# Attention and feed-forward on one core: the first two query blocks of batches 0 and 1 ahead of their later blocks, with feed-forward pieces cut to match

## The chip, the core and the metric

The kernel runs on one core of a Trainium2 chip. The core has five engines, each with an instruction queue of its own that is worked off in order: TensorE (PE in the profile), VectorE (DVE), ScalarE (ACT), GpSimd (POOL) and SyncE (SP). SP does no arithmetic; it issues DMAs. An engine that has to wait for another waits with everything that stands behind in its queue. The metric is the device time of one execution in microseconds: median 402.34 us of three runs (401.5 to 403.08).

## What is computed

A forgetting attention over 8 batches, 8 heads, 576 positions, 64 features, and then a bilinear feed-forward over its 4608 output tokens:

```python
scores = scale * np.matmul(q, k.transpose(0, 1, 3, 2))
cum = np.cumsum(log_f, axis=-1)
decay = cum[:, :, :, None] - cum[:, :, None, :]
scores = np.where(causal, -1000000000.0, scores + decay)
attn = softmax(scores)
attn_out = np.matmul(attn, v)
x = attn_out.transpose(0, 2, 1, 3).reshape(B * S, H * D)   # 4608 x 512
out = ((x @ w_a) * (x @ w_b)) @ w_out                      # w_a, w_b: 512 x 1536
```

## The kernel before

**Recording and order.** The program first records about 2300 operations, each a small function with an engine (or a choice of engines), and then emits them in the order of a table of numbers, ORDER; the string CHOICE gives the engine where there is a choice. Nothing is scheduled when it runs: each engine gets its instructions in the order of the table, and semaphores are set for the data and the buffers. So ORDER decides what stands ahead of what in every queue.

**Attention.** A number t counts pairs of heads, four to a batch (batch b has t = 4b to 4b+3), and u counts half batches (two pairs). The 576 query rows of a head are five blocks i = 0 to 4 (the last of 64 rows), and a causal block i needs keys 0 to i only. They are worked on in four groups g: blocks 1 and 0 together (g = 0), 2, 3 and 4. `qk_group` (L389) puts the scores of one group of one half batch into PSUM; `do_max` (L483), `do_exp` (L539, ACT), `do_recip` (L554) and `do_norm` (L561, POOL) make P of it. In batches 0 to 2 ("direct") the decay is added by PE, and the maximum is a DVE reduction (L488); from batch 3 on DVE adds the decay from a tile `spread` (L512). P is kept as blocks of 128x128 and has to be transposed for P times V: by a DMA on SP's queue (`do_tr`, L583), or by PE against an identity with an eviction by ACT or DVE (`pe_tr`, L591). Parts of P are called A0 (blocks 0 and 1, 6 squares), A1 (block 2, 6 squares), B (blocks 3 and 4, 13 squares), and A is A0 and A1 together. `values` (L788) records the transposes and P times V: in batches 0 and 1 apart for rows (0, 1), rows (2, 3) and block 4 (L623, L636); in the later batches all at once (L611, L613). `turns` (L785) names the parts that PE transposes. The result is evicted into xT, the transposed input of the feed-forward.

Batches 0 and 1 are recorded by `attention_by_blocks` (L765), which goes group by group over both halves, so that their first blocks can be finished before their later ones.

**Feed-forward.** `ffn(t0, n)` (L922) is one piece of n tokens from token t0 on (batch b holds tokens 576b to 576b+575). It has 12 steps fb: four matmuls psa and four psb (L874), a copy of psa by ACT or DVE (L138 or L142), a product by DVE into ht (L890). Then, for each 128 tokens, three parts of four matmuls pso (L899), a copy and a store. Psa, psb, pso, the transposes by PE and P times V share one ring of four PSUM banks ("ff"). A piece needs the attention of all its tokens. The pieces before are (0, 256), (256, 256), (512, 256), (768, 384), and then seven from token 1152 on with 512 tokens (the last 384). `chain` (L918) keeps the recorded order of all feed-forward matmuls.

**Other work.** q, k and v are loaded by SP (`load_qk`, L288; `load_v`, L272), cast mostly by POOL (L140, L142) and q and k transposed by DVE (L302). The three weights are loaded by POOL's queue (`weights`, L355), w_a and w_b in two pieces each (512 and 1024 columns), w_out in three. Forty `filler` operations (L175) of four small matmuls each have no use but to keep PE busy.

## Time and profile before

| what | value |
|---|---|
| runs | 401.5, 403.08, 402.34 us; median 402.34 |
| span of the profiled execution, first to last instruction | 400.7 us |
| median of the runs over this span | 1.6 us |
| mean granted TensorE clock | 0.986 |
| busy: PE, DVE, ACT, POOL | 383.2, 315.3, 250.0, 253.6 us |
| instructions: PE, DVE, ACT, POOL | 4040, 907, 757, 424 |
| DMA | 78.22 MB in 148311 packets |

The time of the profiled execution is known by its span alone; the runs stand 0.8 to 2.4 us above it. "Busy" of PE counts a matmul until its modelled end, and ends overlap the next matmul, so a busy PE need not be at its peak. Where the text speaks of full pace it goes by the distance between starts of matmuls.

### The profile page before, as it was taken

What the parts mean: (1) busy time and instruction counts of PE and PEld (TensorE: products, weight loads), DVE (VectorE), ACT (ScalarE), POOL (GpSimd) and SP (SyncE); (2) the same over time, 40 slices, a digit from 0 to 9 for tenths busy, and PEclk for the clock granted to TensorE, in tenths of its full rate; (3) what the DMA queues carried; (4) which work ended last, traced back from release to release, by engine and by line L of the source; (5) the groups of instructions that cost most, each with busy time, mean ns of one, the idle gap of its engine ahead of it and who ended that gap; (6) DMA issues with size and microseconds to landing.
All of it is one profiled execution on the core that took longest, in us unless ns stands there. A gap on an engine that the chain in (4) does not pass through costs nothing.

```text
span 400.7 us, 11076 instructions
## 1 busy us (share of the span) xinstructions
PE 383.2 (96%) x4040; PEld 212.0 (53%) x4040; DVE 315.3 (79%) x907; ACT 250.0 (62%) x757; POOL 253.6 (63%) x424
## 2 busy tenths in 40 slices
PE   8598799998999999999999999999999999999996
PEld 7466576765855544454445454544444444444553
DVE  8989798976778988997988889898969892373560
ACT  5798766666667778758785777577868673300011
POOL 3889876887397876897896849787968553000000
PEclk9889999998999999999999999999999999999999
DMA  7999989989999999999999999999997729000102
GB/s 282 240 186 289 204 177 224 213 150 215 208 301 208 227 171 330 201 277 212 295 187 286 211 255 273 233 241 190 276 187 218 157 66 202 28 2 36 71 0 79
DMA packets 148311, 78.22 MB, mean 195 GB/s; under 512 B 130592, under 2 KB 133408, under 8 KB 148256
## 3 DMA queue, kind: packets, MB, share of 16 engines
q1 hardware_dynamic: 144272, 72.53, 77.4%
q0 software_dynamic: 3696, 4.72, 7.0%
q8 instruction: 31, 0.51, 0.5%
q10 hardware_dynamic: 288, 0.26, 0.2%
q14 instruction: 24, 0.20, 0.1%
HBM read 49.69 MB, written 9.58 MB: 148 GB/s over the span
## 4 chain that ended last, share of the span: by engine, by line
PE 79%; DMA 9%; DVE 4%; POOL 2%; ACT 2%; issue 2%; SPq 0%; POOLq 0%; DVEq 0%; ACTq 0%
PE pso L899 22%; PE psa L874 22%; PE psb L874 21%; PE sc L401 8%; DMA wa<-in_moe_w_a_dram 5%; PE pv L611 2%; DVE st L488 2%; DMA k<-in_k_dram 1%; PE pv L613 1%; PE sc L636 1%; DMA PTB<-spread 1%; DMA PTB<-PB 1%; DVE qT L302 1%; PE pv L623 1%; ACT PB L550 1%
## 5 line engine op out<-in xcount | busy, mean ns | idle before, releaser
L874 PE MATMUL psa<-xT,wa 128*128 128x512 f16 (+2 forms) x528 | 116.2, 343 | 2.3 <-DMA wa<-in_moe_w_a_dram 1.7
L874 PE MATMUL psb<-xT,wb 128*128 128x512 f16 (+2 forms) x528 | 116.2, 343 | 0.1
L899 PE MATMUL pso<-wout,ht 128*128 128x512 f16 (+1 forms) x444 | 98.4, 374 | 0.0
L567 POOL TENSOR_SCALAR PA<-PA,st 128x128 f16<-128x128 f16 (+2 forms) x162 | 76.0, 482 | 31.8 <-DVE st L559 20.4
L890 DVE TENSOR_TENSOR ht<-psb,a 128x512 f16<-128x512 f32 (+2 forms) x132 | 76.2, 589 | 22.0 <-PE psb L874 15.0
L512 DVE CUSTOM_DVE_ANT_0 S<-sc,spread 128x128 f32<-128x128 f32 (+3 forms) x160 | 86.7, 567 | 7.7 <-PE sc L401 5.4
L138 ACT CAST a<-psa 128x512 f16<-128x512 f32 (+2 forms) x85 | 43.5, 515 | 55.9 <-PE psa L874 53.8
L874 PEld LDWEIGHTS <-wa 128*128 128x128 f16 x528 | 50.1, 99 | 45.5 <-issue 3.7
L874 PEld LDWEIGHTS <-wb 128*128 128x128 f16 x528 | 50.4, 99 | 41.5 <-issue 1.7
L567 POOL TENSOR_SCALAR PB<-PB,st 128x512 f16<-128x512 f16 (+1 forms) x84 | 58.7, 712 | 15.7 <-DVE st L559 14.6
L550 ACT ACTIVATE PA<-S,st 128x256 f16<-128x256 f32 (+2 forms) x120 | 59.9, 502 | 12.5 <-DVE st L512 12.4
L899 PEld LDWEIGHTS <-ht 128*128 128x128 f16 x444 | 41.7, 98 | 46.8 <-issue 1.3
L488 DVE TENSOR_REDUCE st<-sc 128x2 f32<-128x512 f32 (+7 forms) x68 | 46.3, 723 | 6.0 <-PE sc L401 5.3
L401 PE MATMUL sc<-kT,qT 32*128 32x128 f16 (+5 forms) x960 | 41.7, 272 | 5.5 <-ACT PA L550 2.1
L550 ACT ACTIVATE PB<-S,st 128x512 f16<-128x512 f32 x40 | 28.5, 714 | 7.9 <-DVE st L512 7.9
L401 PEld LDWEIGHTS <-qT 32*128 32x128 f16 (+1 forms) x960 | 18.6, 96 | 26.7 <-issue 14.4
L142 DVE CAST a<-psa 128x512 f16<-128x512 f32 (+2 forms) x47 | 26.2, 560 | 7.2 <-PE psa L874 6.6
L559 DVE RECIPROCAL st<-st 128x2 f32<-128x2 f32 x128 | 18.5, 157 | 14.0 <-ACT PA L550 8.7
L142 POOL CAST k<-k 128x1152 f16<-128x1152 f32 (+1 forms) x15 | 20.5, 1367 | 8.9 <-DMA k<-in_k_dram 8.9
L138 ACT COPY osb<-pso 128x512 f32<-128x512 f32 (+1 forms) x22 | 12.4, 570 | 19.9 <-PE pso L899 15.1
L138 ACT CAST xT<-pv 128x512 f16<-128x512 f32 (+2 forms) x39 | 17.0, 446 | 11.8 <-PE pv L636 5.8
L140 POOL TENSOR_SCALAR q<-q 128x1152 f16<-128x1152 f32 (+1 forms) x15 | 20.6, 1372 | 5.0 <-DMA q<-in_q_dram 4.2
(98 smaller groups left out, 491.5 us busy)
## 6 DMA issues: line engine op xcount, KB each, us to landing
spread<-cum_d SPq DMA_DIRECT2D x20, 576.0 KB, 5.9
out_dram<-osb SPq DMA_DIRECT2D x35, 256.0 KB, 3.8
q<-in_q_dram SPq DMA_DIRECT2D x15, 576.0 KB, 7.3
k<-in_k_dram SPq DMA_DIRECT2D x15, 576.0 KB, 5.2
v<-in_v_dram SPq DMA_DIRECT2D x32, 256.0 KB, 6.1
wout<-in_moe_w_out_dram POOLq DMA_DIRECT2D x3, 512.0 KB, 8.7
v<-in_v_dram SPq DMA_DIRECT2D x8, 128.0 KB, 7.2
wb<-in_moe_w_b_dram POOLq DMA_DIRECT2D x1, 1024.0 KB, 13.5
```

What stands on the lines that cost most here:

```text
L138: nc.scalar.copy(out=out_, in_=in_)
L140: ENG[e].tensor_scalar(out=out_, in0=in_, scalar1=0.125, scalar2=1.0, op0=MUL, op1=MUL)
L142: ENG[e].tensor_copy(out=out_, in_=in_)
L401: nc.tensor.matmul(out=dst, lhsT=lhsT, rhs=rhs, start=start, stop=stop, skip_group_check=True)
L488: nc.vector.tensor_reduce(out=m if i == 4 else st[:, 2 * i:2 * i + 2][:, h:h + 1] if isinstance(x, list) else m, in_=y, axis=AXX, op=MAX, ...
L512: nc.vector.tensor_tensor_reduce(out=o, in0=x, in1=y, scale=-1.0, scalar=3e38, op0=ADD, op1=MIN, accum_out=m)
L550: nc.scalar.activation(out=p_blocks(t, i)[:, :, h, :], in_=x.rearrange("p (j k) -> p j k", k=128), func=EXP, scale=sign, bias=st[:, c:c + ...
L559: nc.vector.reciprocal(out=st[:, 20 + 2 * i:22 + 2 * i], in_=st[:, 10 + 2 * i:12 + 2 * i])
L567: ENG[e].tensor_scalar(out=p, in0=p, scalar1=st[:, c:c + 1], scalar2=1.0, op0=MUL, op1=MUL)
L874: nc.tensor.matmul(out=o, lhsT=w16[:, db, 128 * fb:128 * fb + 128], rhs=tokens(db, t0, n), start=(db == 0), stop=(db == 3))
L890: nc.vector.tensor_tensor(out=ht[:, 0:n], in0=T.pop(("psb", t0, fb))[:, 0:n], in1=T.pop(("a16", t0, fb))[:, 0:n], op=MUL)
L899: nc.tensor.matmul(out=o, lhsT=T[("ht", t0, fb)][:, 128 * tb:128 * tb + 128], rhs=wout16[:, fb, c], start=(fb == 0), stop=(fb == 11))
```

## The change

Five things change, and the table ORDER with them.

1. PE now transposes part A0 of batches 0 and 1 only; A1 and B of batch 0 go to DMA transposes on SP's queue, and batch 1's A0 comes from there.
2. The early feed-forward pieces are (0, 256), (576, 256), (256, 320), (832, 320): the first two blocks of batch 0, the first two of batch 1, and then the rest of each. A piece of 320 tokens ends in a half block of 64 tokens, which `ff_out` computes as two matmuls of 64 rows and 256 columns into the two halves of one PSUM tile; two small stores follow. The piece for token pairs (PAIR), which nothing used, is gone.
3. w_a and w_b are loaded in three pieces of 512 columns, and the first no longer waits for the cast of v.
4. Only the first group of u = 1 still takes single PSUM banks of the ring "ff" for its scores (`single`); its groups 1 and 2 take two-bank tiles as the others do.
5. psa/psb and pso are chained apart, so a later piece's psa may stand ahead of an earlier piece's pso.

```diff
-        for lo, hi in ((0, 512), (512, DF)):
+        for lo, hi in ((0, 512), (512, 1024), (1024, DF)):
...
-            if not w_ops:
-                o.deps.append(v_ops[0][0])
...
-        return u == 1 and g < 3
+        return u == 1 and g == 0
...
-        return (b, part) in {(0, "A0"), (0, "A1"), (0, "B")}
+        return (b, part) in {(0, "A0"), (1, "A0")}
...
+            if half:
+                for x in range(2):
+                    nc.tensor.matmul(out=o[HP[x], :], lhsT=T[("ht", t0, fb)][:, 128 * tb:128 * tb + 64],
+                                     rhs=wout16[:, fb, 256 * x:256 * x + 256], start=(fb == 0), stop=(fb == 11),
+                                     skip_group_check=True)
+                continue
...
-    last_ff = []
-
-    def chain(o):
-        o.after.extend(last_ff[-1:])
-        last_ff.append(o)
+    last_ff = {"h": [], "o": []}
+
+    def chain(o, row):
+        o.after.extend(last_ff[row][-1:])
+        last_ff[row].append(o)
...
-        for tb in range(n // 128):
-            end = t0 + 128 * tb + 128 == NT
-            for c in (slice(0, 256), slice(256, 512)) if end else (slice(0, 512),):
+        for tb in range((n + 127) // 128):
+            end, half = t0 + 128 * tb + 128 == NT, n < 128 * tb + 128
+            for c in (slice(0, 256), slice(256, 512)) if end else (slice(0, 256 if half else 512),):
...
-    for t0, n in [(0, 256), (256, 256), (512, 256), (768, 384)] + [(1152 + 512 * n, 512 if n < 6 else 384) for n in range(7)]:
+    for t0, n in [(0, 256), (576, 256), (256, 320), (832, 320)] + [(1152 + 512 * n, 512 if n < 6 else 384) for n in range(7)]:
...
-        42-44 0 20 41 2 1 64 26 31 23 54 55 45 16 32 13 12 71 46 37 47 56 18 67 27 65 34 72 73 68 48 24 19
+        0 24 20 42 71 14 67 43 44 1 64 54 45 46 41 72 47 79 48-50 55 65 56 57 73 74 28 10 36 68 69 51 70 98
```

What the table does is seen in the queues. SP's queue from the load of batch 2's first k on, before (an xT target is a part A0 or A1 of batch 1, PTB a part B; L456 loads `spread`, L914 stores an output block):

```order
L288 DMA k_1459<-in_k_dram 128x1152
L583 DMA_TRANSPOSE xT_67<-S 128x6x128
L272 DMA v_1553<-in_v_dram 128x8x64 x2
L288 DMA k_1610<-in_k_dram 128x1152
L456 DMA spread_80<-cum_d 128x2x576
L288 DMA q_1619<-in_q_dram 128x1152
L583 DMA_TRANSPOSE xT_66<-PA 128x6x128
L914 DMA out_dram<-osb 128x512
```

The same place in SP's queue now, where the transposes are parts of batch 0 (PTB is part B of a pair, xT its part A1):

```order
L288 DMA k_1081<-in_k_dram 128x1152
L581 DMA_TRANSPOSE PTB<-PB_76 128x13x128
L581 DMA_TRANSPOSE xT_67<-PA 128x6x128
L272 DMA v_1261<-in_v_dram 128x8x64 x2
L272 DMA v_1375<-in_v_dram 64x8x64
L581 DMA_TRANSPOSE PTB<-PB_77 128x13x128
L581 DMA_TRANSPOSE xT_66<-PA 128x6x128
L272 DMA v_1479<-in_v_dram 128x8x64 x2
L581 DMA_TRANSPOSE xT_69<-spread_80 128x6x128
L581 DMA_TRANSPOSE xT_68<-spread_79 128x6x128
L581 DMA_TRANSPOSE PTB<-spread_80 128x13x128
L581 DMA_TRANSPOSE PTB<-spread_79 128x13x128
```

Eight DMA transposes of batch 0 (four of part B, four of A1) with the late v loads of batches 0 and 1 stand there now. The rest of batch 2's loads, which stood there, and batch 1's own transposes come behind them.

POOL's queue at the weights, before (L567 normalizes P; wa and wb are the weights w_a and w_b):

```order
L365 DMA wa_70<-in_moe_w_a_dram 128x4x512
L567 TENSOR_SCALAR PA<-PA,st 128x2x128 x2
L365 DMA wb_71<-in_moe_w_b_dram 128x4x512
L567 TENSOR_SCALAR PA<-PA,st 128x128
L142 CAST nv_74<-v_377 128x1024
L567 TENSOR_SCALAR spread_80<-spread_80,st 128x2x128
L365 DMA wb_71<-in_moe_w_b_dram 128x4x1024
L365 DMA wa_70<-in_moe_w_a_dram 128x4x1024
```

and now, at the place where the second and third piece of w_b are issued (the first piece of w_b and all three of w_a stand 5 to 15 rows ahead of the first row shown):

```order
L140 TENSOR_SCALAR q_543<-q_408 128x1152
L565 TENSOR_SCALAR PA<-PA,st 128x128
L565 TENSOR_SCALAR spread_80<-spread_80,st 128x2x128
L565 TENSOR_SCALAR PA<-PA,st 128x128
L565 TENSOR_SCALAR spread_80<-spread_80,st 128x2x128
L565 TENSOR_SCALAR spread_80<-spread_80,st 128x128 x2
L565 TENSOR_SCALAR spread_79<-spread_79,st 128x128 x2
L365 DMA wb_71<-in_moe_w_b_dram 128x4x512
L565 TENSOR_SCALAR spread_79<-spread_79,st 128x3x128
L365 DMA wb_71<-in_moe_w_b_dram 128x4x512
```

All of w_a is issued early, in equal pieces; two thirds of w_b are issued only behind the last normalization of batch 0's first two blocks.

More of the change, by code (lines that the diff above doesn't have):

```diff
@@ L892, in ff_mul, with ff_out @@
         T[("ht", t0, fb)] = ht
-    def ff_out(t0, tb, part, c):
+    def ff_out(t0, tb, part, c, half):
         if part == 0:
@@ L905, in ff_ocopy, with ff_store @@
         T[("osb", t0, tb, c)] = osb
[L907 removed]
+    def ff_store(e, t0, tb, c, half):
         r0 = t0 + 128 * tb
[L909 to L912 removed]
+        if half:
+            y = T.pop(("osb", t0, tb, c))
+            for x in range(2):
+                ENG[e].dma_start(out=out[r0:r0 + 64, 256 * x:256 * x + 256], in_=y[HP[x], 0:256])
             return
         ENG[e].dma_start(out=out[r0:r0 + 128, c], in_=T.pop(("osb", t0, tb, c))[:, 0:c.stop - c.start])
[L916 to L920 removed]
+    last_ff = {"h": [], "o": []}
+    def chain(o, row):
+        o.after.extend(last_ff[row][-1:])
+        last_ff[row].append(o)
     def ffn(t0, n):
         need = set()
[L924 removed]
+        for tok in range(t0, t0 + n, 64):
             b, i = tok // S, (tok % S) // 128
@@ L966, in ffn @@
                 ou = take(oc, "osb")
-                so = op("SA" if end else "S", "sto", lambda e, tb=tb, c=c: ff_store(e, t0, n, tb, c), [oc], w)
+                so = op("SA" if end else "S", "sto", lambda e, tb=tb, c=c, half=half: ff_store(e, t0, tb, c, half), [oc], w)
                 ou.append(so)
```

140 lines of the change are left out of this document (85 added, 55 removed), and 91 rows, old and new, of the table ORDER.

## The prediction

> **What bounds the kernel now.** I read the busy times by stretches first, then the chain of work that ended last, then single places in the timeline.
>
> Busy time by stretches of the span (start:end, length, then busy us and instructions of each engine, the granted PE clock, the DMA share, GB/s):
>
> ```profile
> core 0: us, PE busy (x) PEld busy (x) DVE busy (x) ACT busy (x) POOL busy (x), PEclk, DMA share, GB/s
> 0.00:20.00 20.00, 13.30 (x216) 11.20 (x217) 17.84 (x47) 13.49 (x41) 12.48 (x29) 0.93 0.89 261
> 20.00:40.00 20.00, 17.93 (x319) 13.33 (x317) 18.32 (x43) 17.19 (x54) 18.06 (x29) 0.90 1.11 237
> 40.00:60.00 20.00, 17.73 (x312) 13.64 (x311) 17.71 (x41) 14.06 (x47) 15.89 (x23) 1.00 0.97 190
> 60.00:80.00 20.00, 19.16 (x317) 13.88 (x315) 18.39 (x47) 13.35 (x48) 14.23 (x24) 1.00 1.14 220
> 80.00:100.00 20.00, 18.23 (x260) 11.99 (x259) 13.05 (x32) 13.11 (x46) 15.46 (x28) 0.91 0.97 180
> 120.00:220.00 100.00, 99.95 (x946) 49.10 (x945) 88.69 (x299) 74.08 (x224) 79.25 (x129) 1.00 1.02 239
> 220.00:320.00 100.00, 100.00 (x886) 46.52 (x885) 86.73 (x291) 73.11 (x220) 75.55 (x128) 1.00 0.97 226
> ```
>
> From 120 us on PE never stops. Until 80 us DVE is busy for some 90% (18.32 of 20), and PE has gaps and a clock below 1. So the kernel has an early part that attention's other engines pace, and a later part that PE paces; the later part can only be shortened by less PE work, the early part by fewer waits.
>
> PE's pace, from the chain of waits in order of time (start, length, what) and from PE's timeline:
>
> ```profile
> 22.51 21.65 DMA wa<-in_moe_w_a_dram
> 55.26 0.91 PE sc L401 x32
> 149.87 0.86 PE psa L874 x4
> 153.70 0.97 PE psa L874 x4
> 363.61 10.36 PE pso L899 x48
> 395.39 2.09 DMA out_dram<-osb
> ...
> 30.37 0.61 PE L874 MATMUL psa<-xT,wa 128*128 128x256 f16 x4
> 147.98 1.03 PE L874 MATMUL psa<-xT,wa 128*128 128x512 f16 x4
> 346.59 0.51 PE L636 MATMUL pv<-PTB,nv 128*64 128x64 f16 x20
> 347.03 1.04 PE L874 MATMUL psb<-xT,wb 128*128 128x512 f16 x4
> 396.77 0.60 PE L899 MATMUL pso<-wout,ht 128*128 128x256 f16 x4
> ```
>
> 48 matmuls of 512 columns take 10.36 us: 0.216 us each, and by columns 0.108 for 256, 0.162 for 384, 0.054 for 128. By this rate 1152 tokens of feed-forward are 70.0 us (46.6 for psa and psb, 108 pso at 0.216), and 3456 tokens 209.8. The 32 matmuls of a score group, which run four abreast, take 0.91.
>
> Two marks cut the span: the first psa of the first piece at 30.37 us, and the first psa of the piece at token 1152 at 147.98. **Behind the second mark** stand 209.8 us of feed-forward, 14.2 of scores and 13.5 of P times V (20 pairs, each 0.135 for block 4 and 0.54 for the rest): 237.5. The last matmul ends at 397.4, so they took 249.4: 1.05 times. The chain shows why: a group of four takes 0.86, but 0.97 where another shape follows. **Between the marks** stand 70.0 of feed-forward, 16.5 of scores, 7.5 of P times V, 76 transposed squares at 0.054 (4.1) and nine fillers at 0.22 (2.0): 100.0, at 1.05 that is 105.0, and they took 117.6. So **12.6 us are waits and slow clock**, and this is what the change can win. Sum: 30.4 + 105.0 + 12.6 + 249.4 + 3.3 (the end, mostly the last store) = 400.7, the span. The median run is 402.34, 1.6 more, and I add that at the end.
>
> Where the 12.6 lie, by the same count between places of the order: 5.6 up to the first pso (57.4), 0.7 up to batch 2's first scores (77.5), 3.3 up to the piece at 512 (95.6), 2.7 up to the piece at 768 (119.8), 0.3 after. In the first of these DVE paces, and one weight load is late; in the others PE waits for transposes by DMA and then runs with a slow clock:
>
> ```profile
> PE pv L636 <- DMA PTB<-spread: 1.8, 1, 1.8
> PE psa L874 <- DMA wa<-in_moe_w_a_dram: 1.7, 1, 1.7
> 95.58 0.93 PE L874 MATMUL psa<-xT,wa 128*128 128x256 f16 x4
> 96.30 1.06 PE L874 MATMUL psb<-xT,wb 128*128 128x256 f16 x4
> ```
>
> (the first two are rows of who waited for whom up to 120 us: total, times, longest). At 96.30 a group of 256 columns takes 0.85 until the next starts, twice its 0.43.
>
> **The change part by part.**
>
> *Transposes by PE.* 52 squares fewer (76 go, 24 for batch 1's A0 come): 52 x 0.054 = 2.8 us of PE less, all of it between the marks. Twelve evictions go and four come; the sixteen of now are some 10 us of DVE and ACT, so about 5 us go from them. On SP's queue four transposes of 6 squares and four of 13 come, and four of 6 go:
>
> ```profile
> L583 SPq DMA_TRANSPOSE PTB<-PB x26: 1285/1539/3816, 70.2 to 335.4; - x26
> L583 SPq DMA_TRANSPOSE xT<-spread x4: 1238/1284/3030, 81.0 to 88.0; - x4
> DMA to landing us min/median/max: 2.8/4.4/7.2
> 70.19 6.36 SPq L583 DMA_TRANSPOSE PTB<-PB  x2
> ```
>
> (ns, min/median/max of the issue). Net four of 13 squares: by the median 4 x 1.54 = 6.2 us of SP's queue, by the two at 70.19, where the queue is crowded, 4 x 3.18 = 12.7. Behind a transpose that waits for its P stand all later loads, and behind the P times V on PE that waits for its landing stands the whole feed-forward. The cover is the piece (576, 256), whose twelve steps stand between batch 0's last scores and its late P times V: 15.5 us of PE against an issue and a landing of 4.4. I cost this at nothing for batch 0 and at 3 us for batch 1, whose eight transposes meet batch 2's loads; if the cover is gone, it is the 6.2 to 12.7.
>
> A rule speaks against this part. The Trainium skill, "VectorE: DVE Perf Modes", section "The three transpose paths", gives 390 ns for a 128x128 transpose by TensorE and 1309 ns by DMA, and advises TensorE where PSUM will do; by that the 52 squares would be an estimated 68 us of DMA. Here 13 squares land a median 4.4 us after their issue, at most 0.34 us each, so the trace doesn't bear the figure out for whole parts.
>
> *Weights.* The wait of 1.7 us for w_a's second piece (21.65 us in the chain) goes, since that piece is half as long and issued earlier. What is late next is w_b's second piece: POOL issues it behind the first blocks' normalizations, some 28 to 29 us, a piece of this size lands 7.9 us later, and PE wants it at its fifth step, about 34.5.
>
> ```profile
> wa<-in_moe_w_a_dram POOLq DMA_DIRECT2D x1, 512.0 KB, 7.9
> ```
>
> So up to 2 us of wait stay here; I take 2.
>
> *Pieces.* The columns stay the same. Two half blocks replace one block; 20 matmuls of 64 columns on half the array took 0.44 us at 346.59, 0.022 each where 64 columns at full rate are 0.027, so halves run abreast and a half block costs 1.3 us, half of 2.6. If they did not, it would be 2.6 more in all; I take 0. Two stores of 64 rows more are off the path.
>
> *Order.* Up to the piece (256, 320) DVE has the setup (10 us), batch 0 (24), batch 1 but for the maxima of blocks 3 and 4 (15), two transposes for batch 2 (2.4) and two pieces (7.5 each):
>
> ```profile
> L302 DVE STREAM_TRANSPOSE kT<-k 128x576 f32<-128x576 f32 x16 | 19.3, 1210 | 0.0
> L488 DVE TENSOR_REDUCE st<-sc 128x2 f32<-128x1024 f32 x10 | 11.8, 1217 | 1.5 <-PE sc L401 1.5
> L488 DVE TENSOR_REDUCE st<-sc 128x2 f32<-128x768 f32 x10 | 9.2, 949 | 0.6 <-PE sc L401 0.6
> L488 DVE TENSOR_REDUCE st<-sc 128x1 f32<-128x576 f32 x12 | 8.5, 747 | 1.0 <-PE sc L401 1.0
> L488 DVE TENSOR_REDUCE st<-sc 128x2 f32<-128x512 f32 x10 | 6.7, 670 | 1.3 <-PE sc L401 1.3
> L488 DVE TENSOR_REDUCE st<-sc 128x2 f32<-128x256 f32 x10 | 4.1, 413 | 0.6 <-ACT spread L550 0.6
> L890 DVE TENSOR_TENSOR ht<-psb,a 128x256 f16<-128x256 f32 x36 | 14.7, 418 | 6.5 <-ACT a L138 2.6 <-PE psb L874 2.5 <-PE pv L623 0.6
> L142 DVE CAST a<-psa 128x256 f16<-128x256 f32 x17 | 7.0, 415 | 1.7 <-PE psa L874 1.7
> ```
>
> (a batch: four pairs with 4.0 us of maxima each, 20 reciprocals at 0.16, four transposes at 1.21; a piece: 12 products and half of 12 copies). Sum 66, at 90% busy 73 us. PE has 41.4 us of work from its first psa to there, at 1.05 43.5, so it comes there at 73 too: the second piece gives PE 15.5 us of work for 7.5 of DVE, where attention gives 8.5 for 24. That is the gain of the order: DVE no longer paces. In the kernel before, PE had done 6 us less work by 73 us. The first psa needs 26 us of DVE work ahead where it needed 27.5, so I take 29.4 for 30.4.
>
> *Fillers.* Twenty stand ahead of the first psa, nine between the marks as before, and eleven behind the second, where none stood and PE has no gap: 11 x 0.22 = 2.4 us lost.
>
> **The sum.** Between the marks: 70.0 + 15.4 (scores: some of batch 3's groups now stand behind the second mark) + 7.5 + 24 squares 1.3 + 2.0 = 96.1, at 1.05 100.9. Behind: 209.8 + 15.5 + 13.5 + 2.4 = 241.2, with the 11.9 us of shape changes of now 253.1. Waits: 2 for w_b, 3 for batch 1's transposes, 1.5 for those of batch 2, which now meet less work between: 6.5. So 29.4 + 100.9 + 6.5 + 253.1 + 3.3 = 393.2 us of span, and **394.8 us** with the 1.6.
>
> **The rivals.** *PE alone bounds* (0.12): no waits, 386.7, as a time 388. For it: from 120 us on now PE waits for nothing. Against: nine tenths of DVE are in use early.
>
> *The waits move, but stay* (0.17): 12.6 again, 399.3, as a time 401. Batch 0 now waits for DMA as batch 1 did, and DMA shares are 0.97 to 1.14 early. For it: the wait of 1.8 for PTB, at that very kind of transpose. Against: SP's queue had slack, as it sat waiting for POOL's P, not for DMA (row of who SP waited for, 120 to 320 us):
>
> ```profile
> SPq L583 <- POOL PB L567: 33.5, 16, 6.0
> ```
>
> *Slower: SP's queue becomes the bound* (0.14): eight transposes of batch 0 stand ahead of all late v loads of batches 0 and 1, then batch 2's loads, then batch 1's transposes. If the net four cost their crowded price and nothing covers them, the waits are 12.6 + 6.2 to 12.7, and the end lies at 406 to 412; 408 with 7.5. It decides from 14 us of waits between the marks. The skill's rule on transposes, named above, points this way.
>
> A wait also costs clock, as at 96.30: four groups at twice their time, 1.7 us. The Trainium skill, "TensorE: Matmul & The Clock Gate", section "What's actually happening", has the clock halve after an idle window of about 3.4 us; no filler now stands between the first piece's end and the piece at 832. By the trace that would add 1.7 us to a long wait, and it is within the range.
>
> **How the numbers follow.** Forecast 0.57, the rivals 0.12, 0.17 and 0.14. The range reaches from PE alone, 388, to a slower end short of the crowded price, 406. A difference under 0.5% can't be told from none: faster is below 400.3, slower above 404.4. The forecast, PE alone and a little of the second rival make 0.72 faster; the rest of that and the forecast's upper edge 0.14 same; 0.14 slower.
>
> **What would show it.** Right: the first pso of piece one some 10 us earlier than 57.4; no PE wait for w_a; the first psa of the piece at 1152 near 137, PE without gaps behind it. Wrong: PE waiting for xT or PTB from SP at P times V of batches 0 and 1 for more than 3 us, SP's transposes issued back to back at 3 us each, or PE waits behind 1152, where I have none.

## The result, and the profile after

The changed kernel takes 414.88 us in the median (413.88 to 414.94), the kernel before 402.13 beside it: 1.032 times as long, with a 95% interval from 1.0296 to 1.0345. The prediction was 394.8, with a range up to 406; it was wrong in its sign, and the time lies beyond the range.

Busy time by stretches of the changed kernel (the columns are those of the same view before):

```profile
core 0: us, PE busy (x) PEld busy (x) DVE busy (x) ACT busy (x) POOL busy (x), PEclk, DMA share, GB/s
0.00:20.00 20.00, 12.27 (x164) 8.64 (x165) 15.51 (x38) 11.24 (x31) 13.14 (x30) 1.00 0.89 269
20.00:40.00 20.00, 17.19 (x202) 12.29 (x200) 13.75 (x32) 15.15 (x55) 10.23 (x18) 1.00 1.08 194
40.00:60.00 20.00, 16.72 (x242) 11.75 (x240) 14.99 (x40) 11.19 (x39) 16.99 (x29) 0.91 0.71 140
60.00:80.00 20.00, 20.00 (x293) 14.52 (x282) 15.60 (x35) 14.87 (x43) 11.54 (x17) 1.00 0.92 144
80.00:100.00 20.00, 18.15 (x280) 12.19 (x278) 15.55 (x33) 11.23 (x34) 13.24 (x18) 1.00 1.00 266
120.00:220.00 100.00, 97.28 (x1027) 50.97 (x1025) 85.75 (x272) 70.07 (x216) 73.81 (x124) 1.00 1.06 242
220.00:320.00 100.00, 98.02 (x919) 46.34 (x918) 89.51 (x301) 70.83 (x216) 77.33 (x131) 1.00 0.99 238
```

(The granted clock of 1.00 in the first two rows is no measured grant; see the last section.) Two things are new. DVE, which was 90% busy up to 80 us, is now 75% busy from 20 to 100 us. And PE, which had no gap behind 120 us, now has 2 to 3 us of gaps in each 100.

Places in PE's timeline (start, length, what), first of the kernel before: the first scores of batch 2 (u = 4), of u = 8 and of u = 15; then of the changed kernel, in order of time: the first psa, the first pso, the first psa of the piece (256, 320), batch 2's first scores, the first psa of the piece at 1152, and the first scores of u = 8 and u = 15.

```profile
77.48 0.41 PE L401 MATMUL sc<-kT,qT 32*128 32x128 f16 x14
164.61 0.40 PE L401 MATMUL sc<-kT,qT 32*128 32x128 f16 x16
310.91 0.40 PE L401 MATMUL sc<-kT,qT 32*128 32x128 f16 x15
...
35.90 0.50 PE L865 MATMUL psa<-xT,wa 128*128 128x256 f16 x3
56.59 1.91 PE L896 MATMUL pso<-wout,ht 128*128 128x512 f16 x4
86.77 0.72 PE L865 MATMUL psa<-xT,wa 128*128 128x320 f16 x4
95.59 0.29 PE L399 MATMUL sc<-kT,qT 32*128 32x128 f16 x8
149.17 0.81 PE L865 MATMUL psa<-xT,wa 128*128 128x512 f16 x3
183.33 0.38 PE L399 MATMUL sc<-kT,qT 32*128 32x128 f16 x13
326.21 0.40 PE L399 MATMUL sc<-kT,qT 32*128 32x128 f16 x16
```

Laid side by side, with the last matmul and the span:

| place | before | after | later by |
|---|---|---|---|
| first psa | 30.4 | 35.9 | 5.5 |
| batch 2's first scores (u = 4) | 77.5 | 95.6 | 18.1 |
| first psa of the piece at 1152 | 148.0 | 149.2 | 1.2 |
| first scores of u = 8 | 164.6 | 183.3 | 18.7 |
| first scores of u = 15 | 310.9 | 326.2 | 15.3 |
| last matmul ends | 397.4 | 410.0 | 12.6 |
| span | 400.7 | 413.1 | 12.4 |

By the feed-forward's mark at 1152 the two kernels are level. By attention's places the changed kernel is 18 us late from batch 2 on, and it never makes that up. From u = 8 to u = 15 attention takes 142.9 us for seven half batches, 20.4 each; before it was 146.3, 20.9 each.

What PE waits for behind the mark at 1152 (total, times, longest), 4.1 us in the view's rows where the kernel before has none, and under it what DVE waits for up to batch 2's first scores, before and after:

```profile
PE psa L865 <- DVE ht L881: 1.3, 2, 1.1
PE sc L634 <- DMA PTB<-PB: 1.2, 1, 1.2
PE sc L399 <- DVE qT L302: 0.5, 2, 0.3
...
DVE st L488 <- PE sc L401: 2.1, 4, 0.9
...
DVE st L486 <- PE sc L399: 11.0, 12, 2.0
```

So DVE, which the prediction took for the engine that paces the early part, now waits 11 us for scores there.

### The profile page after: what moved, and what is told of

It reads as the page before. It is cut to its first block, busy times and chain, and to the rows that moved or that the text cites. A ratio compares the mean times of both kernels' runs of the same rounds, so it can differ in the third digit from the quotient of the medians.

```text
span 413.1 us, 11010 instructions
## 1 busy us (share of the span) xinstructions
PE 388.4 (94%) x4024; PEld 213.0 (52%) x4024; DVE 314.2 (76%) x903; ACT 248.1 (60%) x748; POOL 255.7 (62%) x428
## 4 chain that ended last, share of the span: by engine, by line
PE 51%; DVE 19%; DMA 9%; POOL 7%; ACT 7%; issue 5%; POOLq 0%; DVEq 0%; SPq 0%; ACTq 0%
PE pso L896 14%; PE psa L865 12%; PE psb L865 12%; DVE S L510 8%; PE sc L399 7%; DMA PTB<-PB 5%; DMA out_dram<-osb 3%; POOL PB L565 3%; ACT PA L548 3%; DVE ht L881 3%; DVE st L486 2%; POOL PA L565 2%; DVE a L142 1%; PE pv L609 1%; ACT spread L548 1%
## 5 line engine op out<-in xcount | busy, mean ns | idle before, releaser
L865 PE MATMUL psa<-xT,wa 128*128 128x512 f16 (+3 forms) x528 | 115.4, 341 | 2.5 <-DVE ht L881 1.3
L865 PE MATMUL psb<-xT,wb 128*128 128x512 f16 (+3 forms) x528 | 115.2, 340 | 2.5 <-ACT osb L138 1.5
L565 POOL TENSOR_SCALAR PA<-PA,st 128x256 f16<-128x256 f16 (+2 forms) x162 | 75.3, 478 | 38.7 <-DVE st L557 29.7
L881 DVE TENSOR_TENSOR ht<-psb,a 128x512 f16<-128x512 f32 (+3 forms) x132 | 76.0, 588 | 22.0 <-PE psb L865 16.7
L138 ACT CAST a<-psa 128x512 f16<-128x512 f32 (+3 forms) x82 | 42.3, 517 | 57.4 <-PE psa L865 48.7
L486 DVE TENSOR_REDUCE st<-sc 128x2 f32<-128x512 f32 (+6 forms) x64 | 47.5, 763 | 20.2 <-PE sc L399 15.4
L399 PE MATMUL sc<-kT,qT 32*128 32x128 f16 (+5 forms) x960 | 44.5, 281 | 4.3 <-ACT PA L548 2.4
L142 DVE CAST a<-psa 128x512 f16<-128x512 f32 (+3 forms) x50 | 27.9, 558 | 6.2 <-PE psa L865 5.9
L548 ACT ACTIVATE PA<-sc,st 128x256 f16<-128x256 f32 (+2 forms) x42 | 19.4, 473 | 9.8 <-DVE st L486 9.7
L565 POOL TENSOR_SCALAR spread<-spread,st 128x256 f16<-128x256 f16 (+4 forms) x36 | 19.6, 553 | 6.8 <-DVE st L557 6.6
```

What stands on the lines that cost most here:

```text
L138: nc.scalar.copy(out=out_, in_=in_)
L142: ENG[e].tensor_copy(out=out_, in_=in_)
L399: nc.tensor.matmul(out=dst, lhsT=lhsT, rhs=rhs, start=start, stop=stop, skip_group_check=True)
L486: nc.vector.tensor_reduce(out=m if i == 4 else st[:, 2 * i:2 * i + 2][:, h:h + 1] if isinstance(x, list) else m, in_=y, axis=AXX, op=MAX, ...
L548: nc.scalar.activation(out=p_blocks(t, i)[:, :, h, :], in_=x.rearrange("p (j k) -> p j k", k=128), func=EXP, scale=sign, bias=st[:, c:c + ...
L565: ENG[e].tensor_scalar(out=p, in0=p, scalar1=st[:, c:c + 1], scalar2=1.0, op0=MUL, op1=MUL)
```

## The experiments

Eighteen kernels. The table has what was measured; "place" is the start of batch 2's first scores and of those of u = 8 in PE's timeline, "rest" the span less the place of batch 2's first scores. Places, span and rest are of the one profiled run; its time stands up to 3.5 us from the median (e4: 410.4, e8: 419.7).

| kernel | time | ratio to before (95%) | batch 2 | u = 8 | span | rest |
|---|---|---|---|---|---|---|
| before | 402.1 | | 77.5 | 164.6 | 400.7 | 323.2 |
| after | 414.9 | 1.030 to 1.035 | 95.6 | 183.3 | 413.1 | 317.5 |
| e1, fillers in front | 414.8 | 1.027 to 1.038 | 94.1 | 180.9 | 412.2 | 318.1 |
| e3, e1 with the late order of before | 424.7 | 1.051 to 1.060 | 92.1 | 186.2 | 423.3 | 331.2 |
| e4, before with the late order of after | 413.9 | 1.022 to 1.034 | 77.8 | 176.9 | 408.6 | 330.8 |
| e5, e1 with feed-forward 140 places later | 498.2 | 1.235 to 1.245 | 94.0 | 197.6 | 496.1 | 402.1 |
| e6, after, half sums behind 1152 | 398.1 | one run | 94.0 | 180.2 | 396.3 | 302.3 |
| e7, before, half sums behind 1152 | 384.6 | one run | 77.3 | 162.6 | 382.8 | 305.5 |
| e8, after, late copies on ACT | 417.0 | 1.033 to 1.046 | 94.6 | 182.7 | 417.8 | 323.2 |
| e9, after, start of before | 425.2 | 1.054 to 1.066 | 100.6 | 188.6 | 424.3 | 323.7 |
| e11, after, no late transposes by DVE | 413.0 | 1.022 to 1.032 | 93.3 | 180.8 | 413.3 | 320.0 |
| e12, before, the same | 401.9 | 0.997 to 1.003 | 78.1 | 165.4 | 400.9 | 322.8 |
| e13, e7 and the same | 383.3 | one run | 78.1 | 162.4 | 381.5 | 303.4 |
| e14, before, transposes of after | 414.3 | 1.026 to 1.035 | 88.9 | 174.4 | 411.4 | 322.5 |
| e15, e1 with feed-forward a half batch later | 492.7 | 1.217 to 1.232 | 96.5 | 199.1 | 492.5 | 396.0 |
| e16, before, weights of after | 400.6 | 0.993 to 0.999 | 76.8 | 161.8 | 397.9 | 321.1 |
| e17, after, transposes of before | 427.2 | 1.059 to 1.065 | 105.4 | 191.9 | 425.5 | 320.1 |
| e18, after, half sums up to 1152 | 414.7 | one run | 91.9 | 179.8 | 412.9 | 321.0 |
| e19, before, half sums up to 1152 | 403.0 | one run | 78.4 | 163.6 | 401.2 | 322.8 |
| e20, e16, early copies on ACT | 400.3 | 0.992 to 0.999 | 79.2 | 162.8 | 398.9 | 319.7 |

Where ORDER is changed, the diffs show at most one line of the table; those of e3, e5 and e15 are against e1, on which they are built. Where a run takes over the order of another kernel (e3, e4, e9), it takes that kernel's engines (CHOICE) with it.

### The first theories: fillers and a slow clock at the start, and the order behind 1152

The first psa is 5.5 us late, and up to 36 us PE runs its matmuls at half the rate (last section). Theory 1 was that this comes from the fillers, of which only four stand at PE's start, where 16 stood. e1 moves the eleven late ones (37 13 19 12 30 9 15 35 and 11 31 5 in the table, by number) to the front:

```diff
-        0 24 20 42 71 14 67 43 44 1 64 54 45 46 41 72 47 79 48-50 55 65 56 57 73 74 28 10 36 68 69 51 70 98
+        0 24 20 42 71 14 67 43 44 1 64 54 45 46 41 37 13 19 12 30 9 15 35 72 47 79 48-50 55 65 56 57 73 74
```

> The changed kernel with the eleven fillers that stand behind the piece at 1152 moved: eight behind the first four fillers, three ahead of the second group of scores. Theory 1 (PE runs at half rate up to 36 us because only four fillers stand at its start): the first psa at 31 us where it was 35.9, and 2.4 us less behind 1152, so 407 us. Rival 1 (the first psa is late because the scores of the second half batch no longer have banks of their own): the first psa stays at 35 us or later, only the 2.4 us go, 412 us.

Nothing came of it: 414.75 us. The first psa started at 35.8 us, and taking the eleven fillers out of the stretch behind 1152 didn't shorten that either, though they were some 2.9 us of PE's time there, from their starts to the next matmuls'. PE's waits behind the mark (the three largest rows) grew in their place:

```profile
PE sc L399 <- DVE qT L302: 1.7, 2, 1.0
PE sc L634 <- DMA PTB<-PB: 1.2, 2, 0.9
PE sc L634 <- DVE st L557: 0.9, 1, 0.9
```

The view's rows sum to 5.8 us, where they were 4.1. So PE isn't what sets the time there: it fills what is left to it, with fillers or with waits. Theory 1 fell; its rival had the first psa right and the time not, since it too counted the fillers as lost.

e3 and e4 cross the two orders at the mark at 1152. In e3 the order behind the mark is that of the kernel before, in e4 that of the changed kernel.

```diff
-        638 624 587 789 617 620 623 599 600 618 665 667 610 619 632 633 625 642-644 18 1830 1832 791 1831
+        638 624 587 789 617 620 623 599 600 618 665 667 610 619 632 633 625 642-644 18 1819 1824 1828 1829
```

> The kernel with the moved fillers, and behind the mark at 1152 the order of the kernel before; the attention that the kernel before had already done by the mark (63 operations of batch 3) comes first there. Theory 2 (attention is some 17 us late at the mark, and DVE has 10 us less done, whatever the order behind it): the waits of PE behind 1152 stay, 407 us, within 2 of the kernel with the moved fillers alone. Rival 2 (the order behind the mark is worse): PE's waits and shape changes there go, 6 us less than with the moved fillers alone, 401 us.

```diff
-        1832 1835 1836 769-771 764 735 736 730 738 1824 703 765 1828 705 707 820 802 803 731 1833 799 800
+        1832 1824 1828 1833 1834 1829 799 1835 1837 1836 802 1838 1839 1841 1840 1843-1845 1847 1849 1846
```

> The kernel before up to the mark at 1152, and behind it the order of the changed kernel (fillers all ahead of the mark). Theory 2: no waits behind the mark, since attention is ahead, 402 us, within 2 of the kernel before. Rival 2: the 6.9 us of waits and shape changes of the changed kernel appear behind the mark, 408 to 409 us.

Both crossings are as slow as the changed kernel or slower, and neither theory has it. In e4 attention is on time up to u = 7 (142.0 us; before 143.2), and then u = 8 stands at 176.9 where it stood at 164.6: the order of the changed kernel has 120 steps of psa and psb ahead of these scores, that of the kernel before 111, and an engine works its queue in order, so attention that was ahead is held back to its place in the queue. In e3 the 63 operations of attention that come first behind the mark find no feed-forward beside them: the first psa of the piece at 1152 starts at 166.3. What both show is that a lead of attention at the mark is lost, or has to be paid for, where the order puts it elsewhere.

### What paces the part behind 1152

e6 and e7 leave out half of the sums of psa and psb there, in both kernels. Nothing else changes: DVE's, ACT's, POOL's and SP's queues hold the same instructions.

```diff
-        for db in range(4):
+        nd = 2 if t0 >= 1152 else 4
+        for db in range(nd):
```

> The changed kernel with half of the sums of psa and psb left out from token 1152 on (two of the four matmuls of each), which takes 5.5 us of full pace from PE for each half batch behind the mark; every other instruction stays. Measured by the time from the first scores of u = 8 to those of u = 15, seven half batches, 142.9 us in the changed kernel and 146.3 in the kernel before. Theory 3 (behind the mark attention sets the pace by its own chain of scores, exponential, normalization, transpose and P times V, and PE only fills the rest): 138 to 143 us, hardly shorter. Rival 4 (PE sets the pace): 105 to 110 us.

> The kernel before with the same half of the sums left out. It shows attention's own pace in the order of the kernel before, where PE never waits. Theory 3: also 138 to 145 us from the scores of u = 8 to those of u = 15, so the kernel before had no more than 1 us of room for each half batch. Rival 4: 105 to 110 us.

From u = 8 to u = 15 the changed kernel takes 143.4 us (142.9 with whole sums), the kernel before 144.0 (146.3):

```profile
162.58 0.40 PE L401 MATMUL sc<-kT,qT 32*128 32x128 f16 x16
306.58 0.23 PE L401 MATMUL sc<-kT,qT 32*128 32x128 f16 x2
...
180.22 0.38 PE L399 MATMUL sc<-kT,qT 32*128 32x128 f16 x13
323.65 0.35 PE L399 MATMUL sc<-kT,qT 32*128 32x128 f16 x12
```

(the first two are of e7, the others of e6.) 5.5 us of PE's work less for each half batch change attention's pace by 0.3 us in the kernel before and not at all in the changed one. **PE's work paces neither kernel there**: attention's half batches come every 20.4 to 20.9 us, whatever PE has to do besides, also in the kernel before, whose PE never waits. The difference of the two kernels stays with half the work: spans of 396.3 and 382.8, 13.5 apart, where whole ones are 12.4 apart.

This holds up to u = 15 and not behind it. From the first scores of u = 15 to the end of the span the kernel before takes 89.8 us and e7 76.2, so 13.6 of the 17.9 us by which e7 is shorter lie there, where attention runs out and feed-forward is left. In that last part less PE work does shorten the kernel.

Is it DVE? e11, e12 and e13 take DVE's transposes of q and k out of batches 4 to 7 (the scores read older tiles), in the changed kernel, the kernel before, and the kernel before with half sums. e8 gives DVE's copies behind the mark to ACT instead (the letters are the engines, ACT for DVE at 25 of them).

The first three lines are those of e11, e12 and e13, the two below of e8:

```diff
+        if b >= 4:
+            T[("T", which, b)] = T[("T", which, b - 2)]
+            return
...
-        ADDAADAAADDAAADAAADAADAAADADADAAAAADDAAADDAAAADADDDDAADADAAADAAAADADAAS
...
+        ADDAAAAAAAAAAAAAAADAAAAAAAAAAAAAAAADDAAAAAAAAAAAADDDAAAAAAAAAAAAADADAAS
```

> The changed kernel with the 25 copies of psa behind the mark that DVE does given to ACT: some 16 us of DVE's 200 behind the mark. Theory 3a (it is DVE's share of work that sets attention's pace): the waits of PE behind the mark go, 6 to 9 us less, 406 to 409 us. Theory 3b (it is the length of the chain from one half batch to the next, with ACT in it): within 2 us of the changed kernel, or slower, since ACT's copies then stand between exponentials, 414 to 420 us.

> The changed kernel without DVE's transposes of q and k in batches 4 to 7 (the scores there read the tiles of two batches earlier): 16 transposes of 1.21 us, 2.4 us of DVE for each half batch, nothing added elsewhere. Theory 3 with DVE as the engine that sets attention's pace behind the mark: attention catches up, PE's waits behind the mark go, 404 to 409 us. Rival (the chain's length sets it, or PE): 412 to 415 us.

> The kernel before without the same 16 transposes. PE never waits there behind the mark, so by any theory in which PE's work is its bound: 400 to 402 us, no change. If the time falls by more than 3 us, DVE also holds the kernel before back, in a way that its waits don't show.

> The kernel before with half of the sums of psa and psb left out behind the mark (144.0 us from the scores of u = 8 to those of u = 15) and without the 16 transposes of DVE. DVE's load sets attention's pace: 144 less 7 times 2.4, 127 us, at most 132. The chain's length sets it: 141 to 144 us.

DVE's load isn't it: 2.4 us a half batch less changes the kernel before not at all (ratio 0.9999, 0.9967 to 1.0031), the changed one by 1.9 us, which is not clear of the noise (intervals of 1.0216 to 1.0316 and 1.0296 to 1.0345), and with half sums the seven half batches take 142.9 us instead of 144.0. With the copies on ACT (e8) they take 147.1; that run moves work to ACT and doesn't clear DVE by itself, as e11 to e13 do. Busy time from 160 to 300 us of the kernel before, of e7 and of e13:

```profile
160.00:300.00 140.00, 139.95 (x1274) 65.43 (x1266) 122.52 (x411) 101.16 (x305) 111.28 (x183) 1.00 1.01 237
160.00:300.00 140.00, 115.35 (x1110) 51.95 (x1108) 122.62 (x417) 102.26 (x308) 110.70 (x181) 0.96 1.05 242
160.00:300.00 140.00, 112.70 (x1128) 51.15 (x1127) 110.01 (x404) 102.77 (x312) 111.19 (x183) 1.00 1.06 246
```

PE goes from 140 to 115 busy, then DVE from 123 to 110, and attention's pace stays: 20.9, 20.6 and 20.4 us. No engine is full in e13. What is left, by elimination, is a chain of several engines: most likely attention's own, from scores over decay, exponential, normalization, transposes and P times V to the next scores in PE's queue. PE's largest waits in e7 from 160 to 300 us:

```profile
PE sc L401 <- DVE st L512: 7.9, 11, 1.4
PE sc L636 <- DMA PTB<-PB: 5.4, 6, 2.3
PE psa L875 <- ACT a L138: 3.2, 3, 1.7
PE psb L875 <- DVE ht L891: 2.8, 5, 0.8
```

The first two are links of attention's chain. The other two are not: they are the feed-forward's own copies and products, which free its four banks, and with their like they make 9.5 of the view's 24.0 us. e6 and e7 leave them whole, so a part of theirs in the pace is not ruled out. Which link could be shortened was not tried.

### Why batch 2 is 18 us late

e9 gives the changed kernel the start of the kernel before (its order up to the first psa, and the score banks of u = 1):

```diff
-        return u == 1 and g == 0
+        return u == 1 and g < 3
```

> The changed kernel with the order of the kernel before up to the first psa, 31 fillers and the score banks of u = 1 of before with it, the nine fillers between the marks, none behind. Theory 5 (the first psa is late by its order and its banks): first psa at 30 to 31.5 us, and the gain carried to the end, 409 to 411 us. Rival (what is won at the start is lost in the pace of attention behind the mark, as with the moved fillers): the first psa at 31, the end still at 414 to 415 us.

Neither expectation had it, with 425.2 us. The first psa came at 30.2 us, and batch 2 at 100.6, later than in the changed kernel: batch 1's first scores had lost their place (49.6 us, where they were at 33.8). So an early first psa by itself does not bring batch 2 forward.

e5 and e15 put feed-forward later in the order of e1: e5 from the piece at 576 on by 140 places, e15 from batch 1's second scores on by one half batch of attention. So less of it stands ahead of batch 2. Counted in steps, each four matmuls of psa or of psb, it is 59 in the changed kernel, 41 before, 36 and 38 here.

```diff
-        340 421 1646 1648 1647 1649 1650 1652 1651 1653-1655 1658 342 346 1656 1659 1660 153 1657 437 341
+        340 421 342 346 153 437 341 347 87 88 213 231 348 330 331 198 86 193 352 226 359 353 332 192 220 224
```

> The kernel with the moved fillers, and every feed-forward operation from the piece at 576 on put 140 places later in the order (of 2306), so that batch 2's first scores have 36 steps of psa or psb ahead of them (59 in the changed kernel, 41 in the kernel before). Theory 2: batch 2's first scores near 75 us and batch 3's near 122 us, PE's waits behind 1152 gone, 6 to 8 us less than with the moved fillers alone, 399 to 401 us. Rival 3 (the order with the second piece early is better between the marks, and PE only waits elsewhere): what is won behind 1152 comes back as PE waits up to the piece at 256, 407 us or more.

```diff
-        309 185 310 293 406 317 318 265 1631 1634 396 397 303 322 323 325 207 319 436 1636 324 311 1635 407
+        185 310 293 406 1633 317 318 265 303 322 323 325 207 319 436 324 311 407 396 397 305 209 210 312 211
```

> The kernel with the moved fillers, with every feed-forward operation from batch 1's second scores on put later in the order by one half batch of attention (to the same place between the scores of the next half batch), so that u = 7 has 96 steps of psa and psb ahead of it, as in the kernel before, where the changed kernel has 107. Theory 7 (the changed kernel's time is lost because attention stands half a batch too late in the order): the first scores of u = 8 at 165 to 173 us where they were 181, and 400 to 406 us. Rival 8 (attention is late because its early part itself is slow, by transposes through DMA, and the order only fills that time): PE waits up to the piece at 576 grow by as much as attention's place gains, u = 8 at 177 us or later, 412 us or more.

As times both failed (498 and 493 us): attention takes 25 us a half batch in them, since steps that fitted between its scores now stand elsewhere. But they say one thing: with some 20 steps less ahead, batch 2's scores stand at 94.0 and 96.5, where they stood at 94.1 in e1. So e18 and e19 take the work away and leave every place: half of the sums of psa and psb up to token 1152.

```diff
-        for db in range(4):
+        nd = 2 if t0 < 1152 else 4
+        for db in range(nd):
```

> The changed kernel with half of the sums of psa and psb left out up to token 1152 (two of the four matmuls of each); every queue keeps its order. Of the 34.4 us of feed-forward at full pace ahead of batch 2's first scores, 10.6 go from PE. Theory 10 (the new order's attention is slow by itself up to there, and feed-forward only fills PE's time): batch 2's first scores at 91 us or later, where they were 95.6. Rival (they wait for the feed-forward ahead of them on PE): at 83 to 86 us.

> The kernel before with the same half left out up to token 1152: of 22.9 us of feed-forward ahead of batch 2's first scores, 7.6 go from PE. Batch 2's first scores stood at 77.5 us. If attention's chain paces there, as DVE's nine tenths of busy time say: 74 to 77.5 us; if PE does: 69 to 71 us. The difference to the changed kernel stays 15 us or more by theory 10.

First scores of batch 2 in e18 and e19, and what DVE waits for up to there:

```profile
91.93 0.23 PE L399 MATMUL sc<-kT,qT 32*128 32x128 f16 x2
DVE st L486 <- PE sc L399: 10.8, 12, 1.9
...
78.43 0.23 PE L401 MATMUL sc<-kT,qT 32*128 32x128 f16 x2
DVE st L488 <- PE sc L401: 2.6, 4, 0.8
```

Counted again by steps (48 of 0.43 us and 11 of 0.54 in the changed kernel, 41 of 0.43 before, and half of it), 13.3 and 8.9 us of PE's work are gone ahead of these scores, more than the expectations took. In the changed kernel they start 3.7 us earlier, in the kernel before no earlier at all. Of the 3.7 a part is scatter: in e6 and e8, whose early part is the changed kernel's, the place is 94.0 and 94.6. The ends are the same as with whole sums: spans of 412.9 and 401.2. **So the amount of psa and psb sets this place in neither kernel, and in the new order attention is later by itself**: DVE waits 10.8 us for scores with these sums halved, 11.0 with all of them. The matmuls of pso, whole in both runs, were not taken away.

The part on transposes: e14 puts it alone into the kernel before, e17 takes it alone out of the changed kernel.

```diff
-        return (b, part) in {(0, "A0"), (0, "A1"), (0, "B")}
+        return (b, part) in {(0, "A0"), (1, "A0")}
```

> The kernel before, pieces and order as they were, with the change's part on transposes alone: batch 0's A1 and B by DMA, batch 1's A0 by PE. Theory 6 (the DMA transposes are no bound): 399 to 403 us. Rival, the slower case of the prediction (SP's queue): P times V of batch 0 waits for its transposes, 405 to 412 us.

> The changed kernel, order and pieces as they are, with the transposes as in the kernel before: batch 0's A1 and B by PE, batch 1's A0 by DMA. In the order of the kernel before the same exchange took 9 us of PE's time in waits for batch 0's transposes. Theory 9 (the new order covers the transposes, and what it costs is attention's place): 413 to 417 us, no gain. Rival (the transposes by DMA cost time in the changed kernel too): 405 to 410 us.

e14's rival had the way of it, though not the size, and neither expectation of e17 came true. In the order of the kernel before, the exchange costs 12 us: PE waits for three of them (e14, 40 to 80 us), and batch 2's first scores move from 77.5 to 88.9.

```profile
PE pv L623 <- DMA PTB<-PB: 4.1, 1, 4.1
PE pv L623 <- DMA xT<-PA: 3.0, 1, 3.0
...
PE pv L623 <- DMA PTB<-spread: 1.7, 1, 1.7
```

The row of the changed kernel, from 60 to 120 us:

```profile
PE pv L634 <- DMA PTB<-spread: 0.5, 1, 0.5
```

In the new order they cost PE half a microsecond from 60 to 120 us (the one row of that view that names them; it is a wait at 117 us, in batch 1), as the feed-forward stands in between. With PE's own transposes the new order is 12 us slower (e17), and why is not shown: up to batch 2's first scores its rows name 1.9 us of waits at the transposes themselves. So the four kernels make a square: the old order takes 402 us with its own transposes and 414.3 with the new ones, the new order 427.2 and 414.9. The exchange alone costs as much as the whole change, and with the new transposes the new order is neither worse nor better than the old one. Where the moved transposes stand in e14 and e17 was chosen by hand, so the 12 us belong to those places too. How much of the 18 us is the transposes' latency and how much the place of batch 1's first blocks ahead of batch 0's late ones, these runs can't part.

e16 puts the part on weights alone into the kernel before, and e20 gives eleven early copies from DVE to ACT besides.

```diff
-        for lo, hi in ((0, 512), (512, DF)):
+        for lo, hi in ((0, 512), (512, 1024), (1024, DF)):
...
-        AADDDAADADDAAAADDADDDDDADAADDADDADADAAAADAAADADAADAAAADAAAAAADDDAAAAAADADAAAAAAADAADAAAAAADAAAAADAAA
+        AADDDAAAAAAAAAAAAAADDAAAAAAAAADDADADAAAADAAADADAADAAAADAAAAAADDDAAAAAADADAAAAAAADAADAAAAAADAAAAADAAA
```

> The kernel before with the change's part on weights alone: w_a and w_b in three pieces of 512 columns, the second of w_a issued right behind the first of w_b. The 1.7 us of PE's wait for w_a goes. Theory: 400.5 to 402 us, at most 2 us less. Rival: w_b's second piece or the loads behind it on the queue are late in its place, 402 to 405 us.

> The kernel before with the weights in three pieces (400.63 us, batch 2's first scores at 76.8), and the eleven copies of psa that DVE does ahead of batch 2's first scores given to ACT: 4.6 us of DVE, which is busy for nine tenths of that stretch. If DVE's load sets the place of batch 2's first scores, they come 2 to 4 us earlier and the time falls as much, 397 to 399 us. If the chain through ACT does (as the copies behind the mark showed), they come no earlier, 400 to 404 us.

The weights in three pieces are worth some 1.6 us, as the theory had it (0.996, from 0.9933 to 0.9986): 400.6 us, faster than both kernels. The copies bring nothing more, and batch 2's first scores come no earlier (79.2 us, where e16 has them at 76.8). So 4.6 us less of DVE's work do not bring them forward, though DVE is busy for nine tenths of that stretch; as ACT takes the copies up, this does not clear DVE altogether.

**One reading of the table.** In 13 of the 20 rows the span is the place of batch 2's first scores and 317 to 324 us more, though these places lie 29 us apart. The others have an order that moves attention behind it (e3, e4, e5, e15), or half the feed-forward left behind it (e6, e7, e13). That is the mechanism as far as the runs show it: batch 2's attention starts 18.1 us later, runs on at its own pace, and only a little feed-forward that was done early is saved at the end. 18.1 + 0.6 (up to u = 8) - 3.4 (up to u = 15) - 2.7 (from there to the last matmul) = 12.6, the difference of the last matmuls.

## Why the prediction was wrong, step by step

- **What bounds the kernel.** "From 120 us on PE never stops", and so "the later part can only be shortened by less PE work": the rows were right and the inference wrong. An engine without gaps is not thereby the one that paces; e7 takes 25 us of its 140 away and attention's pace changes by 0.3 of 20.9 us. Only behind u = 15 does less PE work shorten the kernel. The part behind 1152 was forecast at 253.1 us from PE's work alone and took 260.9: this step hid that attention's place at the mark decides its end.
- **The order, the step that failed.** The early part was costed by DVE's load: 66 us of work, "at 90% busy 73 us". DVE was 75% busy from 20 to 100 us, and the piece (256, 320) began at 86.8 instead of 73. Load over a busy share taken from another order is no time: the share is what the order makes of it. The view to read was what DVE waits for (2.1 us for scores, then 11.0), and attention's places rather than the feed-forward's. That batch 2's scores had 59 steps of feed-forward ahead of them instead of 41 could be counted in the order; it was not read as a delay of attention. The count alone does not explain the delay either: with 36 steps ahead, or with half the sums, it stays (e5, e18).
- **First psa**: 29.4 forecast from DVE's work ahead of it, 35.9 measured. The first pso, forecast some 10 us ahead of 57.4, started at 56.6. The term of the first psa was mis-sized; by e9, an early one alone would not have brought batch 2 forward.
- **By the marks**: 29.4, 107.4, 253.1 and 3.3 us forecast; 35.9, 113.3, 260.9 and 3.1 measured, 19.9 us more in all. Between the marks the waits and slow clock were 12.4 us by the prediction's own count (113.3 less the 100.9 of work), where 6.5 were forecast; 12.6 had been the kernel before's.
- **Weights**: the wait of 1.7 us goes, right; the 2 us for w_b's second piece didn't come. e16 prices the part at some 1.6 us.
- **Transposes**: nothing for batch 0 and its cover of feed-forward, right as a wait, since no row names one up to 100 us; 3 us for batch 1, too much, as PE waits 0.5 us. That an exchange costs its time through attention's place (e14, 12 us) was not in the sum. The 4.4 us that it took for 13 squares was the median of transposes of all sizes. From 60 to 120 us SP's transposes of all sizes landed near that price after their issue:

```profile
DMA to landing us min/median/max: 3.4/4.6/5.9
```

- **Half blocks** run two abreast, right: 16 of their matmuls took 0.97 us to the next, so 24 of a half block are 1.5 us, where 1.3 was forecast. The row that it argued from, 0.022 us where full rate is 0.027, did not show that.

```profile
118.76 1.04 PE L892 MATMUL pso<-wout,ht 128*64 128x256 f16 x16
119.73 0.72 PE L865 MATMUL psa<-xT,wa 128*128 128x320 f16 x4
```

- **Fillers**: 2.4 us lost behind the mark was wrong in kind. They stood in time that PE would have waited (e1).
- **The rivals.** "The waits move, but stay" is what happened between the marks (12.4 us), with the loss behind the mark left out of it. The slower rival came nearest in size: its 406 to 412 are ends of the span, and the span is 413.1. It had the wrong place: it asked for 14 us of waits between the marks and for SP issuing transposes at 3 us each; neither came. Its mechanism exists, as e14 shows in the old order.
- **The skill's rule on transposes** ("VectorE: DVE Perf Modes"; the prices stand in "The three transpose paths", the preference for TensorE in "Rules for kernel authors") agrees in direction with e14, where the exchange costs 12 us, and not with e17. The 68 us that its figures would give, an estimate, appeared in neither; in e14 P times V waited 8.8 us for three transposes to land.

What stays open: which link sets attention's 20.4 to 21 us a half batch, and which makes it late in the new order's early part. For the one, the runs rule out PE's feed-forward matmuls, DVE's load and the fillers. For the other, they show that halving psa and psb, or an early first psa, does not mend it. The chain of work that ended last, in the changed kernel, points at two places that no run takes up: from 56.2 to 81.5 us it runs along PE's queue without a wait, so PE is not far from setting the place there, and then it goes through an output store, for which ACT's next copy waits, and PE 1.3 us behind it:

```profile
83.96 5.24 DMA out_dram<-osb
89.22 0.59 ACT osb L138
```

The new pieces, the parted chains of feed-forward and the few copies that changed engine (DVE does 50 of the 132 copies of psa, where it did 47) were not tried apart from the order.

## What to carry to other kernels

Before costing a change by the busiest engine, halve that engine's work in one run: an engine can be full without gaps and still not set the pace. Where a chain of several engines paces, follow the places of its first steps through the program: here a delay of 18 us there was still 15 us at u = 15, and feed-forward done early bought little. An order by hand fits the latencies that it was made for: here exchanging one part of the transposes cost 12 us in either direction, and copies given to another engine brought nothing.

## What the runs showed of the hardware

In the changed kernel PE ran at half its rate for most of the first 36 us. The same kind of group of scores, early and later:

```profile
25.84 1.60 PE L399 MATMUL sc<-kT,qT 32*128 32x512 f16 x8
40.71 0.61 PE L399 MATMUL sc<-kT,qT 32*128 32x512 f16 x8
```

The first takes 0.97 us to the next start, the second 0.44. The profile's rows for the changed kernel give a granted clock of 1.00 there, but that is no measured grant: the record of the clock in its trace begins at 35.9 us. In e1 the same group takes 0.97 us too, the record begins at 5.1 us, and the rows read 0.50. The stretch from 15 to 25 us in the changed kernel and in e1 (the clock is the third number from the end):

```profile
15.00:25.00 10.00, 8.04 (x119) 5.23 (x119) 8.22 (x22) 7.25 (x31) 7.16 (x11) 1.00 1.07 202
15.00:25.00 10.00, 8.45 (x123) 5.48 (x122) 8.22 (x23) 7.25 (x32) 7.18 (x11) 0.50 1.10 205
```

So at the start of a profile the rate has to be read from the distance between starts.

The Trainium skill, "TensorE: Matmul & The Clock Gate", section "What's actually happening", has the clock rise after some 3.4 us of sustained work. Here PE worked from 15.6 to 22.3 us, mostly on scores, with gaps of 0.2 and 0.6 us, and from 22.7 to 31.3 without one, and was slow through both. In e1, with 48 matmuls of fillers at the start, the rate doubled at 5.2 us and was half again from 8.6 us on, behind a wait of 1.8.

When the full clock comes differs between executions. In five traces with the same instructions on PE up to 34 us the record begins at 30.3 (e11), 31.6 (e18), 32.6 (e6), 35.9 (the changed kernel) and 36.7 us (e8), and the first psa starts at 34.3, 34.6, 35.1, 35.9 and 36.6. What the half rate costs the whole kernel no run isolates: the first psa of the ten kernels with this start or that of e1 lay between 33.9 and 36.6 us, wherever their ends lay.
